# An attention planner whose ring buffers have fixed tiles, with another clock for VectorE

## The chip, the cores and the metric

The kernel runs on one core of a Trainium2 chip. The metric is the device time of one execution in microseconds (us). The core has engines that run side by side, each with its own queue, in order: PE (TensorE, matrix products), ACT (ScalarE, one function over a tile), DVE (VectorE, elementwise passes, reductions, 32x32 transposes), POOL (GpSimd) and SP, which issues DMAs. They wait for each other by semaphores. PE writes to PSUM, from which ACT and DVE read.

## The reference

Four layers, each added to its input: attention, linear attention, attention, linear attention, with the same weights for each kind. x is 2048 x 512, with 32 heads of 16.

```python
def _A_ref(x, wqkv, wo):
    ...
    scores = jnp.einsum("bhqd,bhkd->bhqk", q, k) * (Dh ** -0.5)
    p = _softmax(scores, axis=-1)
    o = jnp.einsum("bhqk,bhkd->bhqd", p, v)
    return (lambda x, *d: x.transpose(*d))(o, 0, 2, 1, 3).reshape(B, S, D) @ wo
...
x = A_x
x = x + _A_ref(_layernorm(x, axis=-1), A_wqkv, A_wo)
x = x + _B_ref(_layernorm(x, axis=-1), B_wqkv, B_w_phi, B_wo)
x = x + _A_ref(_layernorm(x, axis=-1), A_wqkv, A_wo)
x = x + _B_ref(_layernorm(x, axis=-1), B_wqkv, B_w_phi, B_wo)
```

`_B_ref` makes features from q and k with two softmaxes over each head and multiplies them with v without an exponential for each pair of positions. The change does not touch it.

## The kernel before

**Work of an attention layer.** The 32 heads make 8 head groups of four, and the 2048 queries 4 blocks of 512: 32 groups `G` (`self.groups`). Each goes over 16 key tiles `kt` of 128, and each key tile over two halves of two heads. So there are 32 x 16 x 2 = 1024 tiles of 128 x 1024 scores a layer. `scores` (L1339, L1346) has PE write one tile to PSUM and ACT take its exponential into an SBUF tile `p`. `pvs` (L1388) has PE multiply both halves of a key tile with the values and accumulate over `kt` in a pair of PSUM banks, which a group holds from its first key tile to its last.

**Power tasks.** Some tiles don't go to ACT. `power_task` computes the exponential on DVE with seven passes (six if the scores lie in the double bank): L1358 or L1361 reads the scores from PSUM into `px`, L1364 splits the mantissa into `m`, L1366 the exponent in place, and L1368 to L1374 multiply two polynomials in place with `t`. Most of them read what the pass before wrote. `m` and `t` come from the ring `pp`, `px` from the pool `xp` of three tiles, or from `pp` when the planner finds none of the three free.

**Beside them** run tasks that fill PE and DVE: `octet` projects values, queries and keys of the next eight heads (`values_task`, `kq_task`, `norms_task`), `norm_task` divides a finished group by its sums, `part` and `tail` multiply with the output weights, `stats_task` and `halved` make the next layer's normed input, and in the first attention layer `prep_b`, `prep_rest` and `prep_ao` prepare weights. PSUM has two pairs for all of these (`take`, `freed`): "pm" and "double". The group that accumulates holds one of them, and power tasks compete with the side tasks for the other.

**The order is planned when the program is built.** `attention` simulates the engines. `pe` and `act` are clocks; `look` searches 2.6 us ahead (`AHEAD_US`) for the order of scores, products and side units that loses ACT the least time, with 0.904 us for an exponential (`EXP`). `fetch` models the supply of PE's instructions. `Plan` is the clock of DVE and POOL: a task is a generator that yields ("V", cost, rank, port) ahead of each pass. `advance` picks, among tasks that are ready at the engine's clock, the lowest rank, then the oldest. After a pass it sets `t.ready = self.end + 0.05`, so that a task is not ready at the instant its pass ends, and another that is ready comes in between. The tasks' order there is the order of the DVE instructions in the program.

**The ring.** `pp` has nine buffers of 128 x 1024 floats (`RING4`). The planner holds nine numbers in `slots`, the times from which a slot is free. An exponential takes the smallest (`slots.pop(0)`), a power task takes two or three (`grab`), and products and finished chains give them back (`give`, `slots.append`). The tiles themselves are asked for from the pool, which hands its buffers out in rotation: a tile gets the buffer of the ninth request before it and waits for that buffer's last reader.

**When a power task starts.** `wants` asks for three free slots (four if no `xp` tile is free), a clock of DVE no more than 3 us ahead (`VBUSY`), a group between 1 and 25 (`POWERS` 26), and that the product is not in its last key tiles. The tile is taken `LEAD` = 7 key tiles ahead of the next score, or `MORE` = 10 if another power task runs (`aim`).

Of the kernel before, what the change touches and what calls it, by code (L numbers as in the profile page):

```python
# [66 lines left out]
LEAD = 7  # L67
# [14 lines left out]
PORT = 3.0  # L82
ALIGN = 0.05
# [8 lines left out]
def mha_hedgehog_stack(ctx, tc, x_in, a_wqkv, a_wo, b_wqkv, b_wphi, b_wo, out, shmin=SHMIN):  # L92
# [261 lines left out]
    def peaks(ws):  # L354

        ms = []
        for w in ws:
            for d in range(w.shape[1]):
                yield "V", 0.63, 3
# [25 lines left out]
    def split_parts(w, sc, name, *drams):  # L385

        hl = None
        for d in range(NC4):
            yield "V", 0.88, 3, 1
# [3 lines left out]
            yield "V", 0.75, 3  # L393
# [12 lines left out]
    def prep_ao():  # L406
        ws = []
        yield a1.outer(2)
        a1.grab(2, a1.outers)
# [5 lines left out]
        for i in range(2):  # L415
            for d in range(2):
                if d == 0:
                    yield a1.outer(1)
                    a1.grab(1, a1.outers)
                yield "V", 0.88, 3, 1  # L420
# [3 lines left out]
                yield "V", 0.75, 3  # L424
# [15 lines left out]
    def prep_b():  # L440
# [5 lines left out]
        for i in range(2):  # L446
            for c0 in (0, 2):
                cols = slice(c0 * P, c0 * P + 2 * P)
                yield a1.outer(1)
                a1.grab(1, a1.outers)  # L450
# [5 lines left out]
                a1.grab(2, a1.outers)  # L456
# [22 lines left out]
                a1.spawn(a1.emptied(idx, pst, turned, 0.7))  # L479
# [9 lines left out]
                a1.spawn(a1.emptied(idx, psf, copied, 0.7))  # L489
# [33 lines left out]
    class Norm:  # L523
# [57 lines left out]
        def stats_task(self, t0, n, owner):  # L581
# [3 lines left out]
            for t in range(n):  # L585
                yield "V", 0.7
# [201 lines left out]
    class Plan:  # L788
# [14 lines left out]
        def pull(self, t):  # L803

            while True:
# [11 lines left out]
                if t.need is not None and t.need[0] != need[0]:  # L817
                    t.ready += 0.12
# [3 lines left out]
        def advance(self, until):  # L822

            while True:
# [112 lines left out]
    class LayerA:  # L937
# [65 lines left out]
        def grab(self, n=1, ring=None):  # L1003
            ring = self.slots if ring is None else ring
            for _ in range(n):
                ring.remove(min(ring))

        def give(self, wait=0.1, n=1):
            self.slots += [max(self.plan.now, self.plan.end) + wait] * n

        def give_outer(self, wait=0.1, sent=False):
            self.outers.append(max(self.plan.now, self.plan.end, self.sp if sent else 0.0) + wait)
# [23 lines left out]
        def turned_sum(self, idx, ps, name, rank=0):  # L1036
# [7 lines left out]
            nc.vector.tensor_tensor(half, half, ps[1], ALU.add)  # L1044
            self.freed(idx)
            yield "V", 0.62, max(rank, 0)
# [14 lines left out]
        def kq_task(self, o, j, ten, idx, ps, sqs):  # L1061
# [6 lines left out]
            yield "V", 0.75, 0  # L1068
# [3 lines left out]
            yield "V", 0.75, 0  # L1072
# [9 lines left out]
        def square_task(self, hi, sqs):  # L1082
            yield "V", 0.7, 1, 1
            sqs.append((self.square(hi), self.plan.end + 0.15))

        def norms_task(self, o, i, idx, psn):

            q = self.oct[o]
            for h in range(2):
                yield "V", 0.66, 0  # L1090
# [20 lines left out]
        def norm_task(self, G, idx, acc):  # L1111
# [4 lines left out]
            yield "V", 0.17, 0, 1  # L1116
            rec = sp.tile([P, 16], F32, name="rec")
            nc.vector.tensor_scalar(rec, yt[:, :, 16 * par], 1e-37, None, op0=ALU.max)
            yield "V", 0.25, 0
            nc.vector.reciprocal(rec, rec)  # L1120
            yield "V", 0.42, 0, 1
# [10 lines left out]
            yield "V", 0.7  # L1132
            yb = np_.tile([P, 512], F32, tag="yb", name="yb")
            nc.vector.transpose(yb, yn.rearrange("p a b -> p (a b)"))
            yield "V", 0.43, 1, 1
            dst = np_.tile([P, 2, 512], F16, tag="osp", name="osp")
            nc.vector.tensor_copy(dst[:, 0], yb)
            yield "V", 0.65, 1, 1
# [210 lines left out]
        def power_task(self, G, kt, half, idx, ps, outer):  # L1349

            pt = xp.tile([P, 2, 512], F32, tag="xt", name="px") if outer else pp.tile([P, 2, 512], F32, tag="p", name="px")
            m = pp.tile([P, 2, 512], F32, tag="p", name="pm")
            t = pp.tile([P, 2, 512], F32, tag="p", name="pz")
            yi = pt.bitcast(I32)
            if idx:
                for u in range(2):
                    yield "V", 0.7, 0
                    nc.vector.tensor_scalar(yi[:, u], ps[u], 8192.0, FIELD * 2.0 ** 23, op0=ALU.mult, op1=ALU.add)  # L1358
            else:
                yield "V", 1.2, 0  # L1360
                nc.vector.tensor_scalar(yi, self.pair, 8192.0, FIELD * 2.0 ** 23, op0=ALU.mult, op1=ALU.add)  # L1361
            self.freed(idx)
            yield "V", 0.62, 2, 1
            nc.vector.tensor_scalar(m.bitcast(I32), yi, KEEP, LEADM, op0=ALU.bitwise_and, op1=ALU.bitwise_or)  # L1364
            yield "V", 0.62, 2, 1
            nc.vector.tensor_scalar(yi, yi, POWER, LEADE, op0=ALU.bitwise_and, op1=ALU.bitwise_or)  # L1366
            yield "V", 1.16, 2, 1
            nc.vector.scalar_tensor_tensor(t, m, PA, m, op0=ALU.add, op1=ALU.mult)  # L1368
            yield "V", 1.16, 2, 1
            nc.vector.scalar_tensor_tensor(pt, t, PB, pt, op0=ALU.add, op1=ALU.mult)  # L1370
            yield "V", 1.16, 2, 1
            nc.vector.scalar_tensor_tensor(t, m, PC, m, op0=ALU.add, op1=ALU.mult)  # L1372
            yield "V", 1.16, 2, 1
# [4 lines left out]
            self.give(n=2)  # L1378
# [19 lines left out]
        def part(self, j):  # L1398
# [7 lines left out]
            for t2 in range(2):  # L1406
                r = (4 * j + 2 * t2) * P
                yield self.outer(1)
                self.grab(1, self.outers)
# [11 lines left out]
        def out_task(self, idx, ps, xt, u, r, here, ln=None):  # L1421

            yield "until", lambda: self.plan.now >= here
            for h in range(2):
                yield "V", 0.75, 0
# [11 lines left out]
        def tail(self, j, ob):  # L1437
            ln = Norm([], f"a{self.li}_{j}")
            for t2 in range(2):
                r = (4 * j + 2 * t2) * P  # L1440
                yield self.outer(1)
                self.grab(1, self.outers)
# [16 lines left out]
            for t in (0, 2):  # L1459
# [8 lines left out]
                self.give(1.2)  # L1468
                self.spawn(self.emptied(idx, ps, halved(t), 1.4))
# [59 lines left out]
        def attention(self, extra, nxt):  # L1529
# [27 lines left out]
            estart, slots, acc, pvdone = [], [0.0] * RING4, {}, 0  # L1557
            self.slots, self.outers = slots, [0.0] * OUTER
# [84 lines left out]
            with tc.manual_schedule(engines=COMPUTE):  # L1643
                while pvq or any(s.gens for s in self.streams):
# [16 lines left out]
                    if wants(pe) and min(self.pfree) <= pe:  # L1661
# [4 lines left out]
                        self.grab(1, self.outers if far else slots)  # L1666
                        self.grab(2)
# [6 lines left out]
                        self.spawn(self.power_task(G, kt, 1, idx, ps, far))  # L1674
# [20 lines left out]
                    if pick == "S":  # L1695
# [11 lines left out]
                    elif pick == "V":  # L1707
# [13 lines left out]
                        for h in range(2):  # L1721
                            (self.outers if (G, kt, h) in outer else slots).append(pe + 0.35)
# [725 lines left out]
```

## Time and profile before

| what | value |
|---|---|
| time, median of 3 runs | 2478.2 us (2472.97 to 2481.21) |
| profiled execution, its own time | 2482.15 us |
| its span | 2480.4 us |
| mean granted clock of PE | 0.989 |
| first attention layer, first to last exponential | 71.5 to 1006.6 us |
| second attention layer | 1308.0 to 2227.5 us |

A line of the profile's groups has the source line, the engine, the operation, what it writes and reads, how often it ran; then its busy time and the mean time of one in ns; then the time that the engine stood idle ahead of it, and what ended most of that. A line of a timeline has the start, the length, the engine and the operation; "xN" merges N of a kind that follow each other, and brackets hold the idle time before it. A line of the waits has the engine and line that waited, what it waited for, the total, how many times, and the longest. "issue" is time in which an engine waited for nothing that the profile shows. A line of the windows has the stretch, its length, and each engine's busy time with its instructions.

### The profile page before, as it was taken

What the parts mean: (1) busy time and instruction counts of PE and PEld (TensorE: products, weight loads), DVE (VectorE), ACT (ScalarE), POOL (GpSimd) and SP (SyncE); (2) the same over time, 40 slices, a digit from 0 to 9 for tenths busy, and PEclk for the clock granted to TensorE, in tenths of its full rate; (3) what the DMA queues carried; (4) which work ended last, traced back from release to release, by engine and by line L of the source; (5) the groups of instructions that cost most, each with busy time, mean ns of one, the idle gap of its engine ahead of it and who ended that gap; (6) DMA issues with size and microseconds to landing.
All of it is one profiled execution on the core that took longest, in us unless ns stands there. A gap on an engine that the chain in (4) does not pass through costs nothing.

```text
span 2480.4 us, 113138 instructions
## 1 busy us (share of the span) xinstructions
PE 2296.5 (93%) x51626; PEld 1182.6 (48%) x51626; DVE 1774.8 (72%) x2866; ACT 2097.1 (85%) x2341; POOL 321.8 (13%) x476
## 2 busy tenths in 40 slices
PE   6999999999989999999899999999999999998998
PEld 4545545454544444445354554454454444444543
DVE  8546786868776446789976875986686732579897
ACT  6899999999999999544538999999999999993553
POOL 3000000000000000366440000000000000005553
PEclk9999999999999999999999999999999999999999
DMA  5410521141136421010123003202310531210003
GB/s 190 74 20 8 94 42 46 37 60 46 46 80 174 137 73 62 27 35 18 61 71 56 17 19 48 38 4 46 45 39 12 105 123 60 74 63 26 26 1 112
DMA packets 124034, 143.49 MB, mean 58 GB/s; under 512 B 65192, under 2 KB 70936, under 8 KB 122648
## 3 DMA queue, kind: packets, MB, share of 16 engines
q1 hardware_dynamic: 122360, 133.38, 22.0%
q8 instruction: 406, 6.65, 1.1%
q0 software_dynamic: 1184, 2.77, 0.3%
q14 instruction: 84, 0.69, 0.1%
HBM read 62.16 MB, written 41.94 MB: 42 GB/s over the span
## 4 chain that ended last, share of the span: by engine, by line
ACT 44%; PE 22%; DVE 20%; issue 11%; POOL 2%; DMA 0%; ACTq 0%; DVEq 0%; POOLq 0%
ACT p L1346 42%; PE s L1339 5%; PE pm L1388 5%; PE double L1388 3%; PE double L758 2%; DVE su L1859 1%; DVE yt L2076 1%; PE pbv L1786 1%; PE pk L1786 1%; PE pq L1786 1%; PE pm L758 1%; DVE pz L1372 1%; POOL f L1868 1%; DVE mx L1848 1%; DVE f L1852 1%
## 5 line engine op out<-in xcount | busy, mean ns | idle before, releaser
L1346 ACT ACTIVATE p<-s 128x1024 f32<-128x1024 f32 x1963 | 1814.0, 1070 | 45.9 <-PE s L1339 33.3
L1339 PE MATMUL s<-kq 49*32 49x512 f16 x14848 | 783.2, 381 | 87.7 <-ACT p L1346 64.9
L1339 PEld LDWEIGHTS <-kq 49*32 49x32 f16 x15872 | 381.8, 90 | 741.6 <-issue 622.4
L1388 PE MATMUL double<-p,v 64*32 64x512 f32 (+1 forms) x11392 | 638.3, 494 | 0.7 <-DVE yt L1044 0.7
L1388 PE MATMUL pm<-p,v 64*32 64x512 f32 (+1 forms) x8968 | 512.7, 489 | 2.2 <-issue 2.1
L1388 PEld LDWEIGHTS double<-p,v 64*32 64x32 f32 x11392 | 224.9, 106 | 39.2 <-issue 2.7
L1388 PEld LDWEIGHTS pm<-p,v 64*32 64x32 f32 x8968 | 184.4, 106 | 40.7 <-issue 7.4
L1786 PEld LDWEIGHTS <-xnTa 128*128 128x128 f16 x1152 | 110.7, 98 | 156.4 <-DVE f L1852 28.8
L1868 POOL TENSOR_TENSOR f<-f,su 128x1024 f32<-128x1024 f32 x58 | 112.1, 1932 | 526.2 <-DVE su L1862 511.6
L1426 DVE SCALAR_TENSOR_TENSOR xt<-pm,c_oA,xt 128x512 f32<-128x512 f32 x78 | 58.2, 746 | 119.6 <-PE pm L758 117.1
L1100 POOL PARTITION_ALL_REDUCE nma<-nmx x6 | 4.4, 736 | 1033.0 <-DVE nmx L1097 766.9
L1786 PE MATMUL pbv<-wbv,xnTa 128*128 128x512 f16 x384 | 91.6, 390 | 24.0 <-DVE f L1852 23.9
L1853 ACT ACTIVATE f<-f,c_pB 128x1024 f32<-128x1024 f32 x62 | 70.2, 1148 | 48.2 <-DVE f L1852 48.0
L1368 DVE SCALAR_TENSOR_TENSOR pz<-pm 128x1024 f32<-128x1024 f32 x85 | 103.1, 1216 | 2.5 <-PE double L1388 1.8
L1370 DVE SCALAR_TENSOR_TENSOR px<-pz,px 128x1024 f32<-128x1024 f32 x85 | 103.7, 1223 | 1.1
L1374 DVE SCALAR_TENSOR_TENSOR px<-pz,px 128x1024 f32<-128x1024 f32 x85 | 103.4, 1217 | 1.0
L1372 DVE SCALAR_TENSOR_TENSOR pz<-pm 128x1024 f32<-128x1024 f32 x85 | 103.4, 1219 | 1.0
L1874 ACT ACTIVATE fk<-f 128x1024 f16<-128x1024 f32 x30 | 31.7, 1057 | 74.8 <-POOL f L1868 74.8
L1071 DVE TENSOR_SCALAR tq<-pm,c_qk 128x512 f32<-128x512 f32 x25 | 18.7, 747 | 105.0 <-PE pm L758 104.9
L758 PEld LDWEIGHTS <-wA 64*32 64x32 f16 x4608 | 74.2, 93 | 40.7 <-issue 0.4
L1786 PE MATMUL pq<-wbqk,xnTa 128*128 128x512 f16 x384 | 88.4, 379 | 0.9 <-DVE vt L1813 0.9
L1786 PE MATMUL pk<-wbqk,xnTa 128*128 128x512 f16 x384 | 88.1, 379 | 0.0
(341 smaller groups left out, 3083.6 us busy)
## 6 DMA issues: line engine op xcount, KB each, us to landing
kq<-stg SPq DMA_DIRECT2D x168, 128.0 KB
xd<-xt SPq DMA_DIRECT2D x40, 512.0 KB
xt<-xd SPq DMA_DIRECT2D x40, 512.0 KB
v<-vyt SPq DMA_DIRECT2D x384, 16.0 KB
oD<-osp SPq DMA_DIRECT2D x24, 256.0 KB
ob<-oD SPq DMA_DIRECT2D x24, 256.0 KB
xt<-in_A_x_dram SPq DMA_DIRECT2D x8, 512.0 KB
wbqk<-dBqk SPq DMA_DIRECT2D x16, 256.0 KB
```

The source lines that it names most:

```text
L758: nc.tensor.matmul(ps[h][c, :], w[r, c], x[r], start=(n == 0), stop=(n == of - 1), skip_group_check=True)
L1339: nc.tensor.matmul(banks2[u][32 * c:32 * c + 32, :], self.side(g, half, 64 * u, 0, kt * P + 32 * c, 32), self.side(g, half, 64 * u, 1, j * ...
L1346: nc.scalar.activation(pt, s, AF.Exp, scale=EXPS)
L1368: nc.vector.scalar_tensor_tensor(t, m, PA, m, op0=ALU.add, op1=ALU.mult)
L1370: nc.vector.scalar_tensor_tensor(pt, t, PB, pt, op0=ALU.add, op1=ALU.mult)
L1372: nc.vector.scalar_tensor_tensor(t, m, PC, m, op0=ALU.add, op1=ALU.mult)
L1374: nc.vector.scalar_tensor_tensor(pt, t, PD, pt, op0=ALU.add, op1=ALU.mult)
L1388: nc.tensor.matmul(acc[h][32 * hh:32 * hh + 32, part], self.oct[o]["v"][r, x:x + 32], pt[r, hh % 2, part], start=(kt == 0), stop=(kt == NT ...
L1426: nc.vector.scalar_tensor_tensor(xt[:, u, :], ps[h], con["oA"], xt[:, u, :], op0=ALU.mult, op1=ALU.add)
L1786: nc.tensor.matmul(dst, xnT[:, a, c, t * P:(t + 1) * P], w(b, c), start=(i == 0 and c == 0), stop=(i == 2 and c == NC4 - 1))
L1853: nc.scalar.activation(f, f, AF.Exp, scale=con["pB"])
L1868: nc.gpsimd.tensor_tensor(f3, f3, self.part_sums(f3, slice(0, 64), factor), ALU.mult)
```

## The change

1. *The ring.* At the layer's start nine tiles are taken from `pp`, and each number of `slots` becomes a `Slot`, a number that carries its tile. `grab` returns the tile of the earliest free slot. Exponentials, power tasks and `stats_task` write into the tile that the planner chose, and `give` and the products return that tile. `xp` stays in rotation; its slots carry no tile.
2. *The clock of DVE.* After a pass a task is ready when the engine's clock is (`self.clock[e] = t.ready = at + cost`), so it is among the ready ones for the very next pass. What others may use is 0.09 us later (`DRAIN`).
3. *The costs* of the DVE passes are changed, most of them lower: a power chain's 0.62 and 1.16 to 0.6 and 1.13, and so on.
4. *`LEAD`* goes from 7 to 8.
5. A task that goes from one engine to another is ready 0.25 us later instead of 0.12.

No instruction of the computation is added or removed by the text; how many tiles go to DVE follows from the plan.

```diff
-LEAD = 7
+LEAD = 8
...
+DRAIN = 0.09
...
-            owner.grab()
+            self.xn2[t0 // 2] = owner.grab()
             for t in range(n):
-                yield "V", 0.54
+                yield "V", 0.46
                 self.scaled(t0 + t)
...
                 if t.need is not None and t.need[0] != need[0]:
-                    t.ready += 0.12
+                    t.ready += 0.25
...
-                self.end = self.clock[e] = at + cost
-                t.ready = self.end + 0.05
+                self.clock[e] = t.ready = at + cost
+                self.end = at + cost + (DRAIN if e == "V" else 0.0)
                 self.pull(t)
...
+    class Slot(float):
+        pass
+
+    def slot(at, tile):
+        x = Slot(at)
+        x.tile = tile
+        return x
...
-        def grab(self, n=1, ring=None):
+        def grab(self, ring=None):
             ring = self.slots if ring is None else ring
-            for _ in range(n):
-                ring.remove(min(ring))
-
-        def give(self, wait=0.1, n=1):
-            self.slots += [max(self.plan.now, self.plan.end) + wait] * n
+            n = min(range(len(ring)), key=lambda i: ring[i])
+            return ring.pop(n).tile
+
+        def give(self, tile, wait=0.1):
+            self.slots.append(slot(max(self.plan.now, self.plan.end) + wait, tile))
...
-            yield "V", 0.62, rank
+            yield "V", 0.61, rank
             half = np_.tile([P, 512], F32, tag="yb", name=name + "1", bufs=2)
             nc.vector.tensor_copy(half, ps[0])
-            yield "V", 0.69, rank
+            yield "V", 0.61, rank
             nc.vector.tensor_tensor(half, half, ps[1], ALU.add)
             self.freed(idx)
...
-            yield "V", 0.75, 0
+            yield "V", 0.66, 0
             slot, tq = self.ringed("tq")
...
-            yield "V", 0.43, 1, 1
+            yield "V", 0.34, 1, 1
             nc.vector.tensor_scalar(hi, tq, CLAMP, -CLAMP, op0=ALU.min, op1=ALU.max)
-            yield "V", 0.7, 1, 1
+            yield "V", 0.61, 1, 1
             nc.vector.tensor_tensor(lo, tq, hi, ALU.subtract)
...
         def square_task(self, hi, sqs):
-            yield "V", 0.7, 1, 1
+            yield "V", 0.33, 1, 1
...
-        def scores(self, G, kt, half):
+        def scores(self, G, kt, half, pt):
             s = psS.tile([P, 2, 512], F32, tag="S", name="s")
             self.score_cols(*self.groups[G], kt, half, [s[:, u, :] for u in range(2)])
-            pt = pp.tile([P, 2, 512], F32, tag="p", name="p")
             nc.scalar.activation(pt, s, AF.Exp, scale=EXPS)
...
-        def power_task(self, G, kt, half, idx, ps, outer):
-
-            pt = xp.tile([P, 2, 512], F32, tag="xt", name="px") if outer else pp.tile([P, 2, 512], F32, tag="p", name="px")
-            m = pp.tile([P, 2, 512], F32, tag="p", name="pm")
-            t = pp.tile([P, 2, 512], F32, tag="p", name="pz")
+        def power_task(self, G, kt, half, idx, ps, pt, m, t):
+
+            pt = xp.tile([P, 2, 512], F32, tag="xt", name="px") if pt is None else pt
             yi = pt.bitcast(I32)
...
-                    yield "V", 0.7, 0
+                    yield "V", 0.6, 0
...
-                yield "V", 1.2, 0
+                yield "V", 1.13, 0
...
-            yield "V", 0.62, 2, 1
+            yield "V", 0.6, 2, 1
...
-            yield "V", 1.16, 2, 1
+            yield "V", 1.13, 2, 1
...
-            self.give(n=2)
+            self.give(m), self.give(t)
...
-            estart, slots, acc, pvdone = [], [0.0] * RING4, {}, 0
-            self.slots, self.outers = slots, [0.0] * OUTER
+            estart, slots, acc, pvdone = [], [slot(0.0, pp.tile([P, 2, 512], F32, tag="p", name=f"p{i}_")) for i in range(RING4)], {}, 0
+            self.slots, self.outers = slots, [slot(0.0, None) for _ in range(OUTER)]
...
-                        self.grab(1, self.outers if far else slots)
-                        self.grab(2)
+                        pmz = [self.grab(self.outers if far else slots), self.grab(), self.grab()]
...
-                        self.spawn(self.power_task(G, kt, 1, idx, ps, far))
+                        self.spawn(self.power_task(G, kt, 1, idx, ps, *pmz))
...
-                        self.scores(G, kt, h)
+                        free = slots.pop(0)
+                        self.scores(G, kt, h, free.tile)
                         self.steps += 1
-                        start = max(act, pe + THERE, slots.pop(0))
+                        start = max(act, pe + THERE, free)
...
-                            (self.outers if (G, kt, h) in outer else slots).append(pe + 0.35)
+                            far = (G, kt, h) in outer
+                            (self.outers if far else slots).append(slot(pe + 0.35, None if far else self.pt[(G, kt, h)]))
```

More of the change, by code (lines that the diff above doesn't have):

```diff
@@ L418, in prep_ao @@
                     yield a1.outer(1)
-                    a1.grab(1, a1.outers)
-                yield "V", 0.88, 3, 1
+                    a1.grab(a1.outers)
+                yield "V", 0.42, 3, 1
                 if d == 0:
@@ L1001, in outer @@
             return "until", lambda: sum(x <= self.plan.now for x in self.outers) >= n
-        def grab(self, n=1, ring=None):
+        def grab(self, ring=None):
             ring = self.slots if ring is None else ring
-            for _ in range(n):
-                ring.remove(min(ring))
-        def give(self, wait=0.1, n=1):
-            self.slots += [max(self.plan.now, self.plan.end) + wait] * n
+            n = min(range(len(ring)), key=lambda i: ring[i])
+            return ring.pop(n).tile
+        def give(self, tile, wait=0.1):
+            self.slots.append(slot(max(self.plan.now, self.plan.end) + wait, tile))
         def give_outer(self, wait=0.1, sent=False):
-            self.outers.append(max(self.plan.now, self.plan.end, self.sp if sent else 0.0) + wait)
+            self.outers.append(slot(max(self.plan.now, self.plan.end, self.sp if sent else 0.0) + wait, None))
         def sends(self, cost):
@@ L1039, in turned_sum @@
                 yield self.ring()
-            yield "V", 0.62, rank
+            yield "V", 0.61, rank
             half = np_.tile([P, 512], F32, tag="yb", name=name + "1", bufs=2)
             nc.vector.tensor_copy(half, ps[0])
-            yield "V", 0.69, rank
+            yield "V", 0.61, rank
             nc.vector.tensor_tensor(half, half, ps[1], ALU.add)
             self.freed(idx)
-            yield "V", 0.62, max(rank, 0)
+            yield "V", 0.63, max(rank, 0)
             slot, yt = self.ringed(name + "0")
```

54 lines of the change are left out of this document (27 added, 27 removed).

## The prediction

> **What bounds the kernel now.** I read the page first, then ACT's waits in each attention layer, then ACT's and PE's timelines, and last the VectorE timeline, because the change acts through that engine.
>
> ```profile
> span 2480.4 us, 113138 instructions
> PE 2296.5 (93%) x51626; PEld 1182.6 (48%) x51626; DVE 1774.8 (72%) x2866; ACT 2097.1 (85%) x2341; POOL 321.8 (13%) x476
> ACT 44%; PE 22%; DVE 20%; issue 11%; POOL 2%; DMA 0%; ACTq 0%; DVEq 0%; POOLq 0%
> L1346 ACT ACTIVATE p<-s 128x1024 f32<-128x1024 f32 x1963 | 1814.0, 1070 | 45.9 <-PE s L1339 33.3
> L1368 DVE SCALAR_TENSOR_TENSOR pz<-pm 128x1024 f32<-128x1024 f32 x85 | 103.1, 1216 | 2.5 <-PE double L1388 1.8
> ```
>
> The chain that ended last is led by ACT, and 1963 exponentials (L1346) are nearly all of it. The two attention layers have 2 x 1024 = 2048 exponential tiles; the other 85 are computed on DVE by `power_task` (L1368 counts them). Attention lasts as long as ACT's row of exponentials. These rows of ACT's timeline (start, length, count) are each layer's first and last run; the two rows after them count the exponentials of each layer.
>
> ```profile
> 71.47 1.02 ACT L1346 ACTIVATE p<-s 128x1024 f32<-128x1024 f32 x1 [0.50 <-PE s L1339]
> 869.32 137.26 ACT L1346 ACTIVATE p<-s 128x1024 f32<-128x1024 f32 x149 [1.49 <-PE s L1339]
> 1307.97 1.94 ACT L1346 ACTIVATE p<-s 128x1024 f32<-128x1024 f32 x2 [4.78 <-PE s L1339]
> 2026.41 201.07 ACT L1346 ACTIVATE p<-s 128x1024 f32<-128x1024 f32 x219
> 71.00:1010.00 939.00, 911.07 (x985) 1.00 0.28 65
> 1300.00:2230.00 930.00, 902.97 (x978) 1.00 0.23 50
> ```
>
> A run without a gap gives the exponential's real price: (201.07 - 1.07)/218 = 0.917 us from start to start, although one lasts 1.07: neighbours overlap. Layer one runs from 71.47 to 1006.58, 935.1 us, of which 985 x 0.917 = 903.2 are work: 31.9 us are lost. Layer two: 2227.48 - 1307.97 = 919.5, less 978 x 0.917 = 896.8: 22.7 lost. So all that a better order can save without moving more tiles to DVE is 54.6 us, and each further tile on DVE is worth 0.917. ACT's waits in the two layers, one after the other (us, times, longest), say who causes the loss:
>
> ```profile
> ACT p L1346 <- PE s L1339: 17.0, 27, 2.0
> ACT p L1346 <- DVE px L1374: 3.3, 3, 1.5
> ACT p L1346 <- DVE pz L1372: 2.2, 2, 1.3
> ...
> ACT p L1346 <- PE s L1339: 16.4, 13, 4.8
> ACT p L1346 <- DVE pz L1372: 2.8, 4, 1.3
> ACT p L1346 <- DVE px L1374: 0.2, 1, 0.2
> ```
>
> Waits on L1372 and L1374 are ring waits: an exponential is ready to run, but the buffer that the rotation hands it still belongs to the second-last or last pass of a power chain. One of them, ACT first, then DVE:
>
> ```profile
> 1458.99 43.81 ACT L1346 ACTIVATE p<-s 128x1024 f32<-128x1024 f32 x47 [1.31 <-DVE pz L1372]
> ...
> 1457.67 1.23 DVE L1372 SCALAR_TENSOR_TENSOR pz<-pm 128x1024 f32<-128x1024 f32 x1
> ```
>
> L1372 ends at 1458.90, and the exponential starts 0.09 later. PE, in order, then stood too. PE's own waits over the whole span:
>
> ```profile
> PE s L1339 <- ACT p L1346: 67.2, 175, 1.5
> ...
> PE s L1339 <- issue: 6.4, 7, 1.5
> PE double L758 <- issue: 4.6, 6, 1.5
> ...
> PE pm L1388 <- issue: 2.1, 2, 1.8
> ...
> PE double L1388 <- DVE yt L1044: 0.7, 1, 0.7
> ...
> PE double L1339 <- DVE vyt L1044: 0.2, 1, 0.2
> ```
>
> Two things are to be seen. The stalls named "issue" (13.1 us) wait for no engine, and the edit keeps the planner's model of them (`fetch`), so I leave them. And inside attention PE waits for DVE for only 0.9 us: DVE has been late for ACT, hardly ever for PE.
>
> **The change part by part.**
>
> *Ring buffers.* Before, `pp.tile` gives buffers in rotation, while the planner charges an exponential with the earliest free slot of its list. Now the slot carries its tile. The ten ring waits are 3.3 + 2.2 + 2.8 + 0.2 = 8.5 us, all on ACT, which sets the end. After a wait the overlap is lost too, 1.02 - 0.917 = 0.10 each, 1.0 together. **-9.5** if all go; 0 if the chosen buffer is just as late. What is late next is a score from PE: PE had written its score before each of these waits, as the releaser was DVE, so nothing of the same size stands behind. No instruction or DMA is added; SP's and POOL's queues keep their work, though its places in the order may shift.
>
> *VectorE's clock.* Here is a power chain that ran alone, and then the start of two that ran interleaved:
>
> ```profile
> 325.71 1.19 DVE L1361 TENSOR_SCALAR px<-double 128x1024 int32<-128x1024 f32 x1
> 327.00 0.69 DVE L1364 TENSOR_SCALAR pm<-px 128x1024 int32<-128x1024 int32 x1
> 327.73 0.69 DVE L1366 TENSOR_SCALAR px<-px 128x1024 int32<-128x1024 int32 x1
> 328.34 1.22 DVE L1368 SCALAR_TENSOR_TENSOR pz<-pm 128x1024 f32<-128x1024 f32 x1
> 329.59 1.23 DVE L1370 SCALAR_TENSOR_TENSOR px<-pz,px 128x1024 f32<-128x1024 f32 x1
> 330.85 1.23 DVE L1372 SCALAR_TENSOR_TENSOR pz<-pm 128x1024 f32<-128x1024 f32 x1
> 332.11 1.23 DVE L1374 SCALAR_TENSOR_TENSOR px<-pz,px 128x1024 f32<-128x1024 f32 x1
> ...
> 1381.73 2.35 DVE L1368 SCALAR_TENSOR_TENSOR pz<-pm 128x1024 f32<-128x1024 f32 x2
> 1384.00 2.35 DVE L1370 SCALAR_TENSOR_TENSOR px<-pz,px 128x1024 f32<-128x1024 f32 x2
> ```
>
> Interleaved, two passes take 2.27 us, 1.135 each; the plan's new 1.13 is that distance. In a chain, where a pass reads what the one before wrote, it is 1.25 to 1.26: the write must have ended. So alone the chain needs 7.63 us (325.71 to 333.34). The old clock gave it 1.2 + 2 x 0.62 + 4 x 1.16 + 6 x 0.05 = 7.38; the new one gives 1.13 + 2 x 0.6 + 4 x 1.13 + 0.09 = 6.94. The old clock was 0.25 short for a lone chain; the new one is 0.69 short.
>
> That works in two directions. The plan believes that DVE is free 6% sooner, so it grants more power tasks. A new task needs a free PSUM pair and three free ring slots, and a chain holds two of those slots to its end. With 85 chains, 6% is 5, and each moves 0.917 off ACT. Against it, `LEAD` 8 keeps the result tile one key tile (two exponentials, 1.8 us) longer, and a grant is impossible while slots are short. I bound the count by -4 and +10 and take **+4, -3.7 us**: nearest to the chain's own rows.
>
> *Chains together.* `t.ready` now equals the clock, so a running task is due at once and only a lower rank or an older task displaces it; before, any due task came between. PSUM is freed sooner, as the second read of a pair no longer waits behind a 1.2 us power pass. The price is the distance: 0.12 for each pass that loses its neighbour. At most all 85 chains with five such pairs, 85 x 5 x 0.12 = 51 us of DVE time. DVE, over 24 windows of 40 us in each layer, and in its fullest one, is busy like this (PE, PEld, DVE, ACT, POOL):
>
> ```profile
> sum 960.00, PE 908.54 PEld 469.29 DVE 639.88 ACT 918.73 POOL 18.54; mean PE 37.86 PEld 19.55 DVE 26.66 ACT 38.28 POOL 0.77
> ...
> 1420.00:1460.00 40.00, 37.84 (x1056) 19.00 (x1041) 36.73 (x53) 38.51 (x43) 0.00 (x0) 1.00 0.01 3
> ...
> sum 960.00, PE 903.88 PEld 463.57 DVE 649.70 ACT 912.73 POOL 25.45; mean PE 37.66 PEld 19.32 DVE 27.07 ACT 38.03 POOL 1.06
> ```
>
> DVE idles 13 of 40 us on the mean, and that hides 51 us; in a window like the one at 1420 only 3.3 are left. There it becomes lag: PE's next user of a PSUM pair queues behind its wait, and the scores behind it. Bounds: -3 (pairs freed earlier, as in the few places where PE now waits for DVE, and less loss behind them) to +20 (below). I take **+2**.
>
> The Trainium skill speaks to this term: "VectorE: DVE Perf Modes", section "The DRAIN you can't avoid", reports that eight chained copies cost the same with a semaphore after each as with one at the end. By that, chains would cost nothing extra, this term would be 0 and the sum 2 us lower. The trace disagrees: 1.25 against 1.135.
>
> *LEAD 8.* A power tile is due one key tile later, so its chain has about 1.8 us more. It already had room: the first chain of layer one,
>
> ```profile
> L1388 PEld LDWEIGHTS double<-px,v x480: 102/107/112, 108.0 to 1888.2; 64*32 64x32 f32 x160
> ...
> L1374 DVE SCALAR_TENSOR_TENSOR px<-pz,px x85: 1161/1220/1227, 101.2 to 2007.1; 128x1024 f32<-128x1024 f32 x85
> ```
>
> ended at 102.4, 5.6 us before PE used it. Cost 0; if that room went, PE would wait in line with the scores behind it, which is the slower rival below.
>
> *The rest.* The longer hand-over between engines (0.25 for 0.12) concerns the maximum on POOL, whose rows are awaited tens of us later; weight passes keep the lowest rank; `stats_task` takes its tile from the ring, and the next layer's buffers follow the nine fixed ones in rotation, both behind the last products anyway. Each 0, hidden by exponentials or by the last products; at most one exponential, 0.9, per layer if not.
>
> **Sum:** -9.5 - 3.7 + 2 = -11.2. The profiled execution took 2482.15 us (span 2480.4 and 1.75 around it): 2470.9. It lies 3.95 above the median of 2478.2, so from the median the forecast is **2467**.
>
> **The rivals.**
>
> *Slower: DVE falls behind its clock.* The place is the full stretches. A 40 us window with five lone chains (36.7 us of DVE at 7.63 each) is 5 x 0.69 = 3.5 us longer on the chip than in the plan, and the window at 1420 has 3.3 to spare. If the plan also fills the freed 6% (2.2 us), 3 to 4 us are late per such stretch; with five or six of them some 20 us. Then +20 eats the gain of 13.2 and leaves +7 to +10: 2485 to 2488. It decides from the point where PE's waits for DVE rise from 0.9 to over 13 us. For it: the clock errs the wrong way. Against: PE waits so little now, the plan's own ACT (0.904 a tile) is faster than the chip's 0.917, which gives DVE 1.4% slack, and a stall resynchronizes both.
>
> *Given back.* The freed buffer is one whose power chain has just ended, so the wait returns, and the power count falls by some 3 as tiles live longer: -5 + 2.8 + 1 = -1, **2477**. For it: two of nine slots belong to a chain, and the chain's end in the plan is 0.69 early. Against: the earliest free slot is taken first, and products free two every 1.8 us, so a fresh one is rarely first.
>
> *More power tasks.* If the order lets 12 more tiles through, -9.5 - 11 + 2 = -18.5, **2460**; with part of the 33.4 us of waits on PE's scores saved, down to 2450. For it: strict rank frees PSUM pairs and m, t sooner. Against: the gates on slots stay.
>
> *It does not do what it says:* the slot list and the tiles agree by construction, so the rotation's part can't stay; what can stay is the wait, counted under "given back".
>
> **How the numbers follow.** A measurement of this kernel tells 0.3% (7.4 us) from no change. Forecast (2462 to 2471): 0.38. More power tasks (2445 to 2462): 0.20. Given back (2471 to 2485): 0.27. Slower (over 2485.6): 0.15. Faster by over 0.3% (under 2470.8) is then 0.58, the same 0.27, slower 0.15. The range leaves out a tail of some 0.06 of "more" and of 0.12 of "slower": 2450 to 2487.
>
> **What would show each step.** Ring: no ACT wait for L1372 or L1374 in attention. Count: exponentials on ACT below 1963, near 1959. Chains: L1368, L1370, L1372, L1374 follow each other at 1.25 us oftener. Lag: PE's waits for DVE (vyt, tq, px) of a few us. LEAD: px ends further ahead of its products. I am wrong if ACT still waits for DVE as long as now, if the power count falls, or if PE waits for DVE by over 13 us.

## The result and the profile after

| what | before | after |
|---|---|---|
| median of 5 runs | 2478.2 us | 2490.96 us |
| ratio, 95% interval | | 1.0051 [1.0036, 1.0066] |
| profiled execution, its span | 2482.15, 2480.4 us | 2491.32, 2489.5 us |
| power chains (2048 less the exponentials on ACT) | 85 | 94 |
| first attention layer | 935.1 us | 932.0 us |
| second attention layer | 919.5 us | 928.2 us |
| ACT's waits for DVE in attention | 8.5 us | 1.5 us |
| PE's waits for DVE in attention | 1.7 us | 18.7 us |

The kernel became 0.5% slower, where 0.5% faster was forecast. PE's 1.7 us of before are three waits. The prediction had two of them, 0.9 us, and overlooked this row of the profile before, in layer one:

```profile
PE s L1339 <- DVE nmt L1208: 0.8, 1, 0.8
```

The page after, its first lines and the chain that ended last:

```profile
span 2489.5 us, 113949 instructions
PE 2305.1 (93%) x52042; PEld 1200.5 (48%) x52042; DVE 1877.3 (75%) x2936; ACT 2091.0 (84%) x2332; POOL 327.3 (13%) x476
...
DVE 31%; PE 28%; ACT 27%; issue 8%; SPq 2%; POOL 2%; DMA 1%; DVEq 0%; ACTq 0%; POOLq 0%
```

ACT has less to do than before (2091.0 for 2097.1 us) and leads the chain no more: DVE has 31% of it, 20% before. The windows of ACT's exponentials alone, one row for each attention layer (busy time, count), and then the windows of all engines from each layer's first exponential to the end of its last (PE, PEld, DVE, ACT, POOL):

```profile
60.00:1030.00 970.00, 906.86 (x981) 1.00 0.27 65
1285.00:2270.00 985.00, 901.32 (x973) 0.99 0.22 49
```

```profile
71.97:1004.01 932.04, 886.47 (x24148) 468.63 (x24152) 661.26 (x1029) 906.86 (x981) 14.38 (x23) 1.00 0.27 65
1306.82:2235.07 928.25, 879.31 (x24000) 453.86 (x24000) 669.49 (x969) 901.32 (x973) 10.48 (x19) 1.00 0.23 50
```

981 and 973 exponentials are 9 fewer, worth 9 x 0.917 = 8.3 us. By the sum of the prediction (length less 0.917 for each exponential) layer one loses 932.0 - 899.6 = 32.4 us, 31.9 before, and layer two 928.2 - 892.2 = 36.0, 22.7 before. The waits say what became of it. The exponentials' waits for DVE over the span, and PE's longest for DVE in layer two:

```profile
ACT p__1009 L1354 <- DVE px L1380: 0.9, 1, 0.9
ACT p__27220 L1354 <- DVE p__27219 L1380: 0.4, 1, 0.4
ACT p__27224 L1354 <- DVE vyt L1057: 0.2, 1, 0.2
```

```profile
PE pm L1348 <- DVE yt L1051: 2.1, 2, 1.6
...
PE double L1348 <- DVE tq L1082: 1.8, 4, 0.8
PE pm L759 <- DVE xt L1432: 1.0, 2, 0.5
PE pm L1348 <- DVE yt L1053: 0.8, 2, 0.4
PE pm L1473 <- DVE p__27217 L621: 0.8, 1, 0.8
PE pm L1394 <- DVE tq L1080: 0.8, 1, 0.8
PE pm L1348 <- DVE tq L1082: 0.7, 2, 0.5
```

Of the 8.5 us of ring waits 1.3 are left (L1380). In their place PE waits for DVE, mostly for PSUM pairs that it has not read yet: 17 rows, 12.1 us in layer two, 6.6 in layer one. One such wait, from the timeline of all engines:

```profile
1567.06 1.22 DVE L1376 SCALAR_TENSOR_TENSOR px<-p__27222,px 128x1024 f32<-128x1024 f32 x1
...
1568.32 1.23 DVE L1378 SCALAR_TENSOR_TENSOR p__27222<-p__27219 128x1024 f32<-128x1024 f32 x1
...
1569.57 1.23 DVE L1380 SCALAR_TENSOR_TENSOR px<-p__27222,px 128x1024 f32<-128x1024 f32 x1
...
1570.72 0.68 DVE L1051 COPY yt<-pm 128x512 f32<-128x512 f32 x1
1571.45 0.37 PE L1348 MATMUL pm<-kq 49*32 49x512 f16 x1 [1.57 <-DVE yt L1051]
1571.51 0.69 DVE L1053 TENSOR_TENSOR yt<-yt,pm 128x512 f32<-128x512 f32 x1
...
1572.25 0.41 PE L1348 MATMUL pm<-kq 49*32 49x512 f16 x7 [0.42 <-DVE yt L1053]
...
1572.99 1.02 ACT L1354 ACTIVATE p__27220<-s 128x1024 f32<-128x1024 f32 x1 [1.88 <-PE s L1348]
```

DVE is never idle here. L1051 and L1053 empty the PSUM pair of a finished group, the most urgent passes there are, but they stand behind a chain whose passes run 1.25 apart. PE wants the pair for the scores of the next power task and stands 1.57 and 0.42 us; the exponential behind it comes 1.88 us late. That the chains now stay together shows in the DVE timelines of attention: L1378 is followed at once by L1380 in 89 of 94 chains, the same two passes before in 30 of 85.

### The profile page after: what moved, and what is told of

Its sections match the earlier page's. It is cut to its first block, busy times and chain, and to the rows that moved or that the text cites. A ratio compares the mean times of both kernels' runs of the same rounds, so it can differ in the third digit from the quotient of the medians.

```text
span 2489.5 us, 113949 instructions
## 1 busy us (share of the span) xinstructions
PE 2305.1 (93%) x52042; PEld 1200.5 (48%) x52042; DVE 1877.3 (75%) x2936; ACT 2091.0 (84%) x2332; POOL 327.3 (13%) x476
## 4 chain that ended last, share of the span: by engine, by line
DVE 31%; PE 28%; ACT 27%; issue 8%; SPq 2%; POOL 2%; DMA 1%; DVEq 0%; ACTq 0%; POOLq 0%
PE s L1348 6%; PE pm L1394 6%; PE double L1394 5%; PE double L759 2%; ACT p__1012 L1354 2%; SPq L176 2%; PE pm L759 2%; ACT p__1010 L1354 2%; ACT p__1013 L1354 2%; ACT p__1014 L1354 2%; ACT p__1009 L1354 2%; DVE px L1376 2%; DVE px L1380 2%; ACT p__1007 L1354 2%; ACT p__1011 L1354 2%
## 5 line engine op out<-in xcount | busy, mean ns | idle before, releaser
L1348 PE MATMUL s<-kq 49*32 49x512 f16 x14792 | 798.3, 381 | 68.5 <-ACT p__1009 L1354 5.1
L1354 ACT ACTIVATE p__27218<-s 128x1024 f32<-128x1024 f32 x122 | 129.8, 1064 | 5.7 <-PE s L1348 5.6
L1354 ACT ACTIVATE p__27223<-s 128x1024 f32<-128x1024 f32 x121 | 128.9, 1066 | 3.2 <-PE s L1348 3.0
L1354 ACT ACTIVATE p__1012<-s 128x1024 f32<-128x1024 f32 x117 | 125.7, 1074 | 2.2 <-PE s L1348 2.2
L1354 ACT ACTIVATE p__27220<-s 128x1024 f32<-128x1024 f32 x115 | 122.4, 1064 | 3.1 <-PE s L1348 2.2
L1354 ACT ACTIVATE p__1011<-s 128x1024 f32<-128x1024 f32 x114 | 121.9, 1069 | 3.4 <-PE s L1348 3.3
L1354 ACT ACTIVATE p__1010<-s 128x1024 f32<-128x1024 f32 x113 | 121.0, 1071 | 3.1 <-PE s L1348 3.0
L1354 ACT ACTIVATE p__1006<-s 128x1024 f32<-128x1024 f32 x112 | 120.2, 1073 | 3.1 <-PE s L1348 2.8
L1354 ACT ACTIVATE p__27216<-s 128x1024 f32<-128x1024 f32 x105 | 111.6, 1063 | 8.9 <-PE s L1348 8.7
L1354 ACT ACTIVATE p__27222<-s 128x1024 f32<-128x1024 f32 x109 | 116.4, 1068 | 3.1 <-PE s L1348 2.8
L1354 ACT ACTIVATE p__1009<-s 128x1024 f32<-128x1024 f32 x109 | 116.9, 1072 | 1.9 <-PE s L1348 0.9
L1354 ACT ACTIVATE p__1007<-s 128x1024 f32<-128x1024 f32 x105 | 112.3, 1069 | 5.0 <-PE s L1348 4.8
L1354 ACT ACTIVATE p__1013<-s 128x1024 f32<-128x1024 f32 x107 | 114.6, 1071 | 0.7 <-PE s L1348 0.5
L1354 ACT ACTIVATE p__1008<-s 128x1024 f32<-128x1024 f32 x104 | 111.3, 1070 | 1.3 <-PE s L1348 1.0
L1354 ACT ACTIVATE p__1014<-s 128x1024 f32<-128x1024 f32 x100 | 106.7, 1067 | 4.8 <-PE s L1348 4.3
L1354 ACT ACTIVATE p__27219<-s 128x1024 f32<-128x1024 f32 x102 | 108.8, 1066 | 1.6 <-PE s L1348 1.3
```

What stands on the lines that cost most here:

```text
L1348: nc.tensor.matmul(banks2[u][32 * c:32 * c + 32, :], self.side(g, half, 64 * u, 0, kt * P + 32 * c, 32), self.side(g, half, 64 * u, 1, j * ...
L1354: nc.scalar.activation(pt, s, AF.Exp, scale=EXPS)
```

## The experiments

Theory, formed from these traces: fixed ring tiles gain what was forecast; the new clock charges DVE less than the chip takes, so PSUM pairs come back later than planned, and PE and then ACT wait. Rivals: the fixed tiles cost time themselves; `LEAD` does; the longer distance within a chain does, whatever the clock knows; the new order is worse for PE by itself. "PE for DVE" below is PE's waits for DVE from each attention layer's first exponential to its last, both layers of the profiled execution; "ACT for DVE" is the same for ACT. The kernel before was measured beside each run and took 2478.2 to 2479.8 us, so medians of different rows that lie 2 us apart say nothing.

| kernel | median us | ratio to before, 95% interval | chains | ACT for DVE | PE for DVE |
|---|---|---|---|---|---|
| ring tiles alone | 2469.31 | 0.9955 [0.9939, 0.9971] | 85 | 0 | 3.8 |
| changed, rotation back | 2508.17 | 1.0115 [1.0098, 1.0132] | 94 | 17.0 | 16.6 |
| changed, one pass less | 2475.97 | 0.9989 [0.9977, 1.0] | 94 | 0 | 8.9 |
| ring tiles alone, one pass less | 2468.27 | 0.9949 [0.993, 0.9967] | 85 | 0 | 1.5 |
| changed, chain clock 0.12 | 2495.58 | 1.0069 [1.0055, 1.0083] | 76 | 0 | 13.1 |
| changed, chain clock 0.11 | 2477.63 | 0.9986 [0.9974, 0.9997] | 82 | 0 | 1.9 |
| ring, old costs, chains together | 2487.13 | 1.0035 [1.0019, 1.005] | 83 | 8.7 | 14.9 |
| the same, later release of a store | 2478.66 | 1.0001 [0.9988, 1.0014] | 88 | 0 | 6.1 |
| changed, LEAD 7 | 2494.25 | 1.0058 [1.0039, 1.0077] | 96 | 3.8 | 23.5 |
| ring tiles, hand-over 0.25 | 2474.7 | 0.9983 [0.997, 0.9996] | 86 | 0 | 7.3 |

**Ring tiles alone.** Part 1 of the change on the kernel before; clock, costs and `LEAD` stay.

```diff
+            self.xn2[t0 // 2] = owner.grab()
...
+            n = min(range(len(ring)), key=lambda i: ring[i])
+            return ring.pop(n).tile
...
+                        free = slots.pop(0)
+                        self.scores(G, kt, h, free.tile)
```

> The kernel before with the fixed ring tiles alone: old clock, old costs, LEAD 7. The ring does not enter the planner's clock, so every engine's order is that of before and only the buffers differ. Theory (the change lost its time to a clock of VectorE that runs ahead of the chip): ACT's waits for L1368 to L1374's counterparts fall from 8.5 us to under 1, PE's waits for DVE stay under 3 us, 85 power chains, and the time is 9.5 us below the kernel before, 2465 to 2472. Rival (fixed tiles themselves cost time, by waits that the rotation did not have): the same as before or slower, 2478 and up.

All of PE's waits for DVE in attention, and each layer by engine (as above):

```profile
PE pm L1347 <- DVE yt L1050: 1.1, 1, 1.1
PE s L1347 <- DVE top L1218: 1.0, 1, 1.0
PE pm L1347 <- DVE yt L1052: 0.8, 1, 0.8
PE double L1393 <- DVE yt L1052: 0.7, 1, 0.7
PE double L1347 <- DVE vyt L1052: 0.2, 1, 0.2
```

```profile
71.40:998.13 926.73, 882.59 (x23904) 458.40 (x23904) 616.70 (x999) 909.94 (x985) 10.34 (x23) 1.00 0.28 65
1299.45:2215.88 916.43, 872.50 (x23836) 449.76 (x23840) 613.74 (x933) 902.61 (x978) 9.01 (x19) 0.99 0.23 51
```

985 and 978 exponentials as before, no wait of ACT for DVE, and both layers are shorter, 926.7 for 935.1 and 916.4 for 919.5. The median lies 2479.56 - 2469.31 = 10.2 us under that of the kernel before on the same chip. The ring part is a gain, of the size that its waits had, and this kernel is faster than both.

**The rotation put back** into the changed kernel, whose order stays.

```diff
+            pt = pp.tile([P, 2, 512], F32, tag="p", name="p")
             nc.scalar.activation(pt, s, AF.Exp, scale=EXPS)
...
+            m = pp.tile([P, 2, 512], F32, tag="p", name="pm")
+            t = pp.tile([P, 2, 512], F32, tag="p", name="pz")
```

> The changed kernel with the rotation put back: new clock, new costs, LEAD 8, and the order of every engine that of the changed kernel (94 power chains). Theory: the ring waits of ACT on power chains return, more than the 8.5 us of before, since the chains are more: 10 to 15 us, and the time is 2499 to 2506. Rival (the ring makes no difference in this order, as its waits only move to PE): 2489 to 2493.

ACT's waits for power chains over the span:

```profile
ACT p L1355 <- DVE pz L1381: 10.7, 17, 3.4
ACT p L1355 <- DVE px L1383: 6.3, 20, 1.0
```

17.0 us of ring waits came back, and the time rose by 2508.17 - 2490.96 = 17.2, a little over the upper end of the theory. There are 37 such waits, where the kernel before had ten, so the fixed tiles are worth more in this order than in the old one. So the rest of the change lost not 12.8 us, the difference of the two medians, but 2490.96 - 2469.31 = 21.7, and did so with 8.3 us less work for ACT.

**One pass less.** The changed kernel's plan and order stay; the pass with PC is charged but not issued.

```diff
             yield "V", 1.13, 2, 1
-            nc.vector.scalar_tensor_tensor(t, m, PC, m, op0=ALU.add, op1=ALU.mult)
```

> The changed kernel, its plan untouched, but the chip gets one pass less in each of the 94 power chains: the pass with PC is left out of the computation, while the plan still charges it. DVE's chain is then 1.26 us shorter, 6.4 instead of 7.63, below the 6.94 of the plan. Theory (DVE behind its clock): PE's waits for DVE fall from 18.7 us to under 5 and the time by 10 to 17 us, to 2474 to 2481. Rival (the new order itself is worse for PE and ACT, and the waits for DVE are hidden anyway): within 3 us of 2491.

PE's waits for DVE in layer two, the longest:

```profile
PE pm L759 <- DVE xt L1431: 1.0, 2, 0.5
PE double L1348 <- DVE tq L1082: 0.9, 3, 0.5
PE pm L1472 <- DVE p__27174 L621: 0.8, 1, 0.8
PE double L1348 <- DVE px L1367: 0.7, 1, 0.7
```

The time fell by 15.0 us, as the theory had it, and PE's waits for DVE from 18.7 to 8.9, not under 5: in this layer those for a finished group's pair (`yt`, L1051 and L1053), the longest before, are gone, those for key and query passes (`tq`) fall from 3.7 to 0.9, and those for three others (`xt`, L621, and L1367, the first pass of a chain) hardly change. The order is that of the changed kernel, so the loss is not in the order alone. But 15.0 us are only half of what is missing: this run takes 6.7 us more than ring tiles alone, with 8.3 us less work for ACT.

**The control:** the same pass left out of the kernel with ring tiles alone.

> The control for the run with one pass less: the same pass (with PC) left out of the computation, but in the kernel with the old clock and fixed ring tiles (2469.3 us), its plan untouched. Theory (DVE is behind its clock only under the new clock): PE waits for DVE 3.8 us there already, so the time stays within 3 us of that kernel, 2466 to 2472. Rival (a shorter chain helps any order): 8 to 15 us faster, 2454 to 2461.

1.0 us faster. Under the old clock a pass less in each of 85 chains is worth nothing that can be told from noise. So the length of the chains is on the path in the one order and not in the other.

**A clock that knows chains.** The changed kernel, with the distance in its clock.

```diff
                 e, cost = t.need[:2]
+                if e == "V":
+                    at = max(at, self.clock[e] + DEP) if self.past is t else at
+                    self.past = t
```

> The changed kernel with one thing more in its clock: a pass that follows a pass of its own task starts 0.12 us later, as in the traces (1.25 against 1.13). Chains still stay together, costs and LEAD as changed. The program has 76 power chains instead of 94, which by itself costs ACT 18 x 0.917 = 16.5 us. Theory (the clock's error is what loses): PE's waits for DVE in attention fall from 18.7 us to under 5, so the time falls although ACT has more to do: 2474 to 2482. Rival (the longer distance of chains on the chip is what loses, whatever the clock knows): PE's waits for DVE stay over 10 us and the time is over 2495.

By its numbers this is the rival's outcome: 13.1 us, and 2495.58. But 9.3 of the 13.1 us are a single wait. PE's waits for DVE in layer one, and DVE just before:

```profile
PE double L760 <- DVE xt L1436: 9.3, 1, 9.3
PE double L1398 <- DVE yt L1057: 0.5, 1, 0.5
PE double L1352 <- DVE tq L1086: 0.2, 1, 0.2
```

```profile
762.48 0.49 DVE L394 TENSOR_SCALAR bhl<-bf,sB_sc 128x512 f16<-128x512 f32 x1 [10.29 <-PE s L1352]
```

A weight pass of the lowest rank wanted a large buffer that scores still read, which the plan does not model; everything on DVE stood behind it. Without that wait 3.8 us are left and the time, as an estimate, would be some 2486, with 16.5 us more work for ACT than in the changed kernel. This run does not settle the rival, so the next has nearly as many chains as the kernel before.

> As the run with the chain clock, but with 0.11 us instead of 0.12 for a pass that follows one of its own task; the order comes out with 82 power chains, nearly the 85 of before, so that the count explains little. The 9.3 us that PE lost in one wait in the run with 0.12 (a weight pass on DVE that stood behind a buffer which the plan does not model) need not come again. Theory A (the clock's error is what loses): PE's waits for DVE under 6 us and 2469 plus three exponentials, 2468 to 2478. Theory B (chains by themselves lose): 2483 or more.

PE's waits for DVE in attention, all of them:

```profile
PE s L1352 <- DVE nmt L1221: 0.8, 1, 0.8
PE pm L1398 <- DVE yt L1055: 0.6, 1, 0.6
PE pm L760 <- DVE nm L1104: 0.5, 2, 0.3
```

1.9 us for 18.7, and the median, 2477.63, is at the upper end of what theory A gave, 13.3 under the changed kernel although ACT has 12 exponentials more (11.0 us). Chains stay together here as well (68 of 82), so that alone does not make PE's waits. But the charge also sets how many chains are granted, 82 for 94, and this run does not part the charge from the count. (Its profiled execution, 2471.68, was the fastest of twelve; layers of 926.8 and 910.2 us are therefore not typical, and 1.9 us of waits may not be.)

**Old costs, chains together:** ring tiles, and one line.

```diff
-                t.ready = self.end + 0.05
+                t.ready = self.end
```

> The kernel with fixed ring tiles, old costs, LEAD 7, and one thing more: a task is ready at the instant its pass ends, so chains stay together as in the changed kernel, but each pass is charged at the old, higher cost. 83 power chains. Theory A (the costs, which lie below the chip's, are what loses; chains by themselves are harmless): PE's waits for DVE under 6 us, 2469 plus two exponentials, 2468 to 2476. Theory B (keeping chains together is what loses, by the longer distance on the chip): PE's waits for DVE over 10 us, 2480 or more.

By its numbers this is theory B's outcome: 14.9 us, and 2487.13. But about half of the 17.8 us above ring tiles alone is one place in layer one, where 946.4 us were needed. DVE's first pass of a power chain:

```profile
354.53 1.22 DVE L1366 TENSOR_SCALAR px<-double 128x1024 int32<-128x1024 f32 x1 [9.27 <-DMA dF<-bf]
```

`px` came from the pool `xp`, which still rotates, and its buffer was still being stored to memory. 7.4 us of PE's waits and 8.7 of ACT's follow from it. So that release was planned later:

```diff
                         send(dF[i][:, :, cols], wf)
-                        a1.give_outer(3.0, True)
+                        a1.give_outer(14.0, True)
```

> The run with old costs and chains kept together, with one edit: the plan counts a tile of the pool xp as free 14 us instead of 3 us after the folded weights are sent from it. In that run DVE waited 9.27 us at 345 us for that store, in front of a power chain, PE 7.4 us and ACT 8.7 us behind it. 88 power chains (40 and 48). Theory A (chains kept together are harmless as long as the clock charges them enough; the loss of that run was the store): no such wait, PE's waits for DVE under 7 us in both layers, first attention layer 922 to 930 us long instead of 946, total 2463 to 2473. Theory B (chains by themselves lose): first layer over 935, total over 2480.

The wait is gone, and PE's waits for DVE are 6.1 us; by them theory A holds. By the time, 2478.66, neither does: layer one takes 932.0, between the two bounds, and the kernel is 9.4 us above ring tiles alone, with 2.8 us less work for ACT.

**LEAD 7** in the changed kernel.

> The changed kernel with LEAD back at 7; the order is planned anew and has 96 power chains instead of 94. Theory (the loss is the clock's): within 6 us of the changed kernel, 2485 to 2497, PE's waits for DVE 12 to 25 us. Rival (the longer hold of the px tile is what loses): 2481 or less.

3.3 us slower than the changed kernel, with PE's waits for DVE at 23.5: `LEAD` is not the loss.

**The longer hand-over** on ring tiles alone.

> The kernel with the fixed ring tiles and the old clock (2469.3 us), with the longer hand-over between engines of the change (0.25 for 0.12) and nothing else. The order is planned anew, with 86 power chains instead of 85. Theory (the hand-over has no price; this also shows what a new order by itself is worth): 2463 to 2475. Rival (it belongs to the loss): 2480 or more.

Within the theory's bounds, but 5.4 us above ring tiles alone. The trace has a place of that size in layer one, the weight pass of the run with 0.12 again, and the exponential behind it:

```profile
753.92 0.49 DVE L392 TENSOR_SCALAR bhl<-bf,sB_sc 128x512 f16<-128x512 f32 x1 [16.23 <-PE s L1347]
...
762.02 1.02 ACT L1353 ACTIVATE p__1013<-s 128x1024 f32<-128x1024 f32 x1 [5.13 <-PE s L1347]
```

PE waits 3.7 us for DVE there, half of its 7.3. So, as far as one profiled execution tells (2467.88 us, the fastest of its twelve), the cost is that of an order in which this buffer comes late, and not the hand-over's own.

## Why the prediction was wrong, point by point

- **Bound and losses: right.** ACT's row of exponentials set the length, and its waits for power chains were ring waits: 8.5 us of waits, 10.2 of time.
- **Ring, -9.5: right,** -10.2 measured alone. In the changed order it is worth 17.2.
- **Power count, +4: right in sign, too small.** It was +9, at the upper end of the bounds, and 8.3 us of ACT's work went. None of it reached the time: beside the shorter row of exponentials the loss in the two layers grew from 54.6 to 68.4 us.
- **Lag, +2: the step that failed.** The prediction put it between -3 and +20 and took +2, "DVE idles 13 of 40 us on the mean, and that hides 51 us", with PE's waits of 0.9 us as a sign of room. The mean hides nothing at a hand-over that the plan sets to the instant when a pass should end; how close the plan sets it depends on the clock that was being changed. The two runs with a pass less measure the part that the chains' length makes: 15.0 us under the new clock, 1.0 under the old. The whole rest of the change (clock, costs, `LEAD`, hand-over, more chains) cost +21.7 where -3.7 + 2 = -1.7 was forecast. With the 8.3 us that the count took off ACT, the term that was +2 came to +30.0, over its own upper bound of +20; half of it, 15.0, is shown to hang on the chains' length, and the other half has no run of its own.
- **Why the old clock had room.** The prediction compared one lone chain, 7.38 us charged for 7.63, and called the old clock short. Over all passes it was long. What the planner charges DVE up to its last exponential of each layer, summed while the program is built, beside DVE's busy time in the two layers:

```
                              charged us    busy us                     PE for DVE
before                           1298.9     616.6 + 614.3 = 1230.9      1.7
after                            1241.7     661.3 + 669.5 = 1330.8     18.7
changed, LEAD 7                  1255.6                     1345.6     23.5
changed, one pass less           1241.7                     1218.8      8.9
old costs, later store           1321.1                     1289.1      6.1
changed, chain clock 0.11        1284.1                     1243.4      1.9
```

  Before, most passes ran interleaved at 1.13 and were charged 1.16, others 0.7 for 0.33 (the square): 68 us of reserve. After, chains ran at 1.26 and were charged 1.13, and the two passes that empty a pair, charged 0.61 each, took 0.79 and 0.72 in the timeline at 1570: 89 us short. The 99.9 us more of busy time are 9 chains of some 7.6 us, 68, and by difference the lost overlap. In the last five rows the chains stay together. Ordered by charge less busy time, -90, -89, +23, +32 and +41 us, PE's waits fall to 6.1 and 1.9. They do not follow DVE's load alone: the run with a pass less has the lowest load, and more waits than the two runs below it.

  The Trainium skill ("VectorE: DVE Perf Modes", section "The DRAIN you can't avoid") reports eight copies that take the same time with a semaphore after each as with one after the last. By that, the new charges would have been right for chains too. The rows here differ from it: 1.25 to 1.26 us from start to start in a chain, 1.135 interleaved.
- **LEAD and hand-over at 0:** `LEAD` held (7 is no better). The hand-over's run lies 5.4 us above ring tiles alone, and its trace has 5.1 us of idle time of ACT behind a weight pass that waited for scores in the new order. That "weight passes keep the lowest rank" was no safeguard: DVE takes its passes in the planned order, and all of them stood behind this one.
- **The slower rival had the mechanism right:** PSUM pairs late behind chains, decisive once PE's waits for DVE pass 13 us. They were 18.7. Its price of +20 for the lag was too small, and the result, 2491, lies 3 us above its bound of 2488. Its place, the full stretches, holds for nearly half: cut from each layer's first exponential into windows of 40 us, 13 have DVE busy for over 33 and hold 8.8 us of the waits, and the emptier ones hold the others. One of its figures is a slip: five lone chains are 5 x 7.63 = 38.2 us, and 36.7 is DVE's busy time in the window at 1420. It was given 0.15. Its own trace row, 0.69 us short for each chain, times 94 chains is 65 us; a term with such a size at hand should not have been entered at +2 on the strength of a mean.
- **Buffers at the layers' ends, at most 0.9 each:** outside the two attention layers 2489.5 - 932.0 - 928.2 = 629.3 us are left, 2480.4 - 935.1 - 919.5 = 625.8 before. These 3.5 us were not traced to a cause; in the other runs the same rest is 624.8 to 633.5 us.

**What stays open.** Complete kernels with fixed tiles in which PE waits for DVE 7.3 us or less still range from 2469.3 to 2478.7 us. The two clocks with chains together lie at the upper end of it, and the changed kernel with a pass less, with 8.9 us of waits, is at 2476.0. So it is shown that PE's waits go with a charge that is too low; whether chains together cost time beyond these waits, or whether it is the luck of an order, was not settled.

## What to carry to other kernels

A planner's clock has to charge what the chip takes in the order that this clock brings about: taking a pass at its interleaved distance while an edit keeps dependent passes together plans the hand-overs behind them too early. When an edit changes a clock and a structure at once, measure the structure alone on the old order; here one half was worth -10 us and the other +22. An engine that is idle for over a quarter of the time, as DVE is in attention here, can still set the end, wherever a buffer is planned to come free at the instant when its pass should end.

## What was unexpected

The second attention layer has the same order of PE and DVE in the run with old costs and chains together and in its variant with the later store. Yet it took 914.05 us in the one profiled execution and 920.29 in the other (windows of the layer, one row of each kernel):

```profile
1319.08:2233.13 914.05, 872.92 (x23648) 441.15 (x23642) 647.49 (x946) 901.23 (x976) 10.72 (x19) 1.00 0.23 51
```

```profile
1304.50:2224.79 920.29, 875.64 (x23648) 444.06 (x23648) 647.75 (x946) 902.48 (x976) 10.76 (x19) 1.00 0.23 50
```

PE's waits named "issue" are 2.6 us in the first and 6.1 in the second. A difference of 6 us in one layer of two single profiles is therefore no finding here; only waits that have a row of their own, and medians, are.
